# Attention step of a fused kernel: another order of TensorE's work, k and v transposed by halves, positions by wider matmuls

## The chip, the cores and the metric

The kernel runs on one core of a Trainium2 chip. TensorE does matmuls and transposes, VectorE (DVE), ScalarE (ACT) and GpSimd (POOL) do the rest, and SyncE (SP) issues most transfers. Each engine takes its instructions in the order of its own queue and waits where one of them needs something that another engine has not finished. The metric is the device time of one execution in microseconds; lower is better.

## The reference, cut to what matters

Three parts follow each other: attention over pooled keys and values, a mixture of experts that routes each token to one of eight experts, and a dense layer. The change touches the first part and the routing.

```
k_p = k.reshape(B, H, Sp, pool, D).mean(axis=3)      # B, H, S, D = 8, 8, 576, 64; pool = 8
v_p = v.reshape(B, H, Sp, pool, D).mean(axis=3)
scores = scale * np.matmul(q, k_p.transpose(0, 1, 3, 2))
attn = np.exp(scores - np.max(scores)); attn /= np.sum(attn) + 1e-09
x = np.matmul(attn, v_p)                             # then tokens x (heads*D)
logits = x @ w_gate + modality_bias[modality_id]
e_idx = np.argmax(logits, axis=1)                    # a token goes to expert e_idx
out[mask] = gate_w[mask, None] * (relu(x[mask] @ w1[e]) @ w2[e])
g = h * clip(h + 3, 0, 6) / 6, h = out @ w_in;  y = g @ w_out
```

## The kernel before, in words

Attention works on 36 tiles of 128 tokens with all eight heads. A loop written out in Python makes one step for each tile i, and the queues of TensorE, VectorE, ScalarE and SyncE hold the instructions in exactly the order in which the code names them; only GpSimd's order is left to a scheduler. Nine tiles serve two batches. A step is a software pipeline. Its pieces are called by letters here:

- T, `stage_t(i)`: TensorE transposes the exponentials of tile i in five pieces into `tps`, a PSUM tile of two banks with one buffer (pool `ps_t`). ScalarE copies it out to `eT`.
- E, `stage_e(i + 2)`: ScalarE takes the exponential of the differences `d` of tile i + 2, into `e`.
- X, `stage_x`: ScalarE scales the second half of the weighted sums of tile i - 1 by `rs` into `xg`, in four instructions; this frees the PSUM tile `u1`.
- Q, `stage_q(i + 4)`: four transposes of q into `qps`, one PSUM bank with one buffer (pool `ps_q`), copied out by ScalarE to `qT`.
- S, `stage_s(i + 3)`: scores into two buffers `sps` of `ps_s` (three buffers); VectorE takes the maximum `mx` and the difference `d` of each, four instructions.
- A, `stage_a(i)`: weighted sums into the two PSUM tiles `u0` and `u1`, one buffer each; VectorE then makes `rs` and scales the first half into `xg`.

For each batch b the pooled keys and values `kvq` are prepared once, some steps before its first tile. VectorE sums `kv` down to `kvq` in two stages in different steps. `prep(b)` transposes `kvq` with six transposes into `kvps`, which is a buffer of the same pool `ps_t` that T uses; VectorE copies the keys (partitions 0 to 63 of `kvps`) to one half of `bd`, ScalarE copies the same keys to the other half, then two pieces of `bd` to `bp` (`put_p`), and then the values (partitions 64 to 127) to `vT`. One step later `prep2(b)` multiplies `vT` with the gate's weights (`pw`, twelve matmul records on TensorE), and VectorE and GpSimd fill `vb`. `bd` is what S reads, `vb` what A reads.

Routing goes by nine groups of up to five tiles. `route(j)` lists small VectorE instructions (a reduction `l` over `xg`, maximum, one-hot `oh`, and on ScalarE an exponential `ex`), and `run_fill` puts them singly between the larger VectorE instructions of S and A, four in S and four in A. `route_b` adds the positions in an expert's list: for each tile r of the group it sums the one-hots of the earlier tiles with a matrix of ones and its own with a triangular one, 20 matmuls of 8 columns for a group of five. The rows are then scattered to DRAM by GpSimd. At step 28 `first_x` loads the 400 rows of the first expert (`cxg`), GpSimd scales them by the gate (`gate_x`), and TensorE transposes them between the last tiles. From then on the experts and the dense layer follow, which the change doesn't touch.

Of the kernel before, what the change touches and what calls it, by code (L numbers as in the profile page):

```python
# [19 lines left out]
P = 128  # L20
# [32 lines left out]
PQ = (((2, 3), (3, 4)), ((5, 6), (6, 7)))  # L53
PO = 4
QL = 9
# [18 lines left out]
def attention(tc, g, moe, ins, xr_d):  # L74
# [53 lines left out]
    ones = c1.tile([P, P], BF16, name="ones")  # L128
    nc.gpsimd.memset(ones, 1.0)
    tok = c1.tile([P, NTI], F32, name="tok")  # L130
    t9 = tok.rearrange("p (r t) -> p r t", t=9)
# [49 lines left out]
    def kv_ps():  # L181
        return ps_t.tile([P, 1024], F32, name="kvps", tag="t")
# [25 lines left out]

    def prep(b):
        ps = kv_ps()  # L210
        kv_t(b, 2 * D, ps)
        put_k(b, ps)
        put_p(b)
        put_v(b, ps)

# [145 lines left out]
    def route(j):  # L361
# [4 lines left out]
        t = lambda nm, s_, dt=F32: rp.tile(s_, dt, name=nm, tag=nm)  # L366
        l, ex, w, oh = t("l", sh), t("ex", sh), t("w", sh), t("oh", sh, BF16)
        m, m2 = t("m", [P, n, 1]), t("m2", [P, n, 1])
# [3 lines left out]
        def shift():  # L372
            v.tensor_tensor(l, l, m.to_broadcast(sh), op=ALU.subtract)
            nc.scalar.activation(ex, l, AF.Exp)

# [18 lines left out]
        ]  # L394
        if j >= len(GROUPS) - 3:
            return crit[:5] + rest[:1] + crit[5:6] + rest[1:2] + crit[6:] + rest[2:]
        return crit + rest

    def route_b(new=lambda: ps_s.tile([P, 512], F32, name="rps", tag="s")):
        ops = []  # L400
        for j, (x, oh) in list(rt.items()):
            i0, n = GROUPS[j]
            ps = new()
            for r in range(n + 1):
                for r2 in range(min(r + 1, n)):
                    nc.tensor.matmul(ps[:, r * E:(r + 1) * E], tri if r2 == r else ones, oh[:, r2], start=(r2 == 0),
                                     stop=(r2 == min(r, n - 1)))
            ops += route_c(j, ps, *rt.pop(j))
        return ops
# [67 lines left out]
    sched = {}  # L477
    sched2 = {}

# [60 lines left out]
    for b in range(2, B):  # L540
        for w in range(2):
            for n, rs in enumerate(((4,), (2, 1))):
                at2(PQ[b - 2][w][n] if b < 4 else first[b] - 10 + 2 * w + n, lambda b=b, w=w, rs=rs: pool_kv(b, w, v_, rs=rs))
        if b > 2:
            at(first[b] - 12, lambda b=b: (load_kv(b, 0), load_kv(b, 1)))
            at(first[b] - QL, lambda b=b: load_qs(b))
        o = PO if b == 2 else 6 - b % 2
        at(first[b] - o, lambda b=b: prep(b))
        at2(first[b] - o + 1, lambda b=b: prep2(b))
    at2(ZI, zero_rows)  # L550
# [16 lines left out]
    for i in range(NTI - 3):  # L567
# [6 lines left out]
        if i == XL:  # L574
            each(fill)
            each(fill2)
            del fill[:], fill2[:]
            put_rows()
            tc.add_to_no_dep_group("scatter", moe.first_x())
        stage_t(i)  # L580
# [3 lines left out]
        for j, (a, n) in enumerate(GROUPS):  # L584
            if a + n == i:
                fill.extend(route(j))
        if i > 0 and i + 4 < NTI:
            stage_q(i + 4)
        for fn_ in sched.get(i, ()):
            fn_()  # L590
        stage_s(i + 3)
        if i == NTI - 4:
            sp(-1)
        for fn_ in sched2.get(i, ()):
            fn_()
        fill.extend(route_b())
        stage_a(i)
        if i == 0:
            prep_k(1)
            stage_q(4)  # L600
# [181 lines left out]
def moe1(tc, g, xr_d, tok_d, y_d, s_d, w1, w2, w_in):  # L782
# [71 lines left out]
    def first_x():  # L854
        one = lambda j, hi: nc.sync.value_load(g.one[0:1, j:j + 1], min_val=0, max_val=hi)
        s.e0 = one(0, E - 1)
        r0 = one(1, E * R - R + NW)
        i_ = nc.sync.dma_start(s.xg, xr_d[bass.ds(r0, NW)].rearrange("(t p) x -> p t x", p=T4)).ins
        w_dma(s.e0, 0)
# [436 lines left out]
```

## Time and profile before

| | |
|---|---|
| median of three runs | 1419.65 us (1418.83 to 1419.8) |
| the profiled execution's own time | 1420.61 us |
| its span, first to last instruction | 1418.9 us |
| attention, from the first T to the last | 25.3 to 193.3 us |
| granted TensorE clock, mean of the span | 0.993 |

The profiled execution is 0.96 us longer than the median, and 1.71 us of it lie outside the span. A row of the timeline has the start, the duration, the engine, the line, the operation, output and inputs, the count, and in brackets the idle time before it with what ended it. TensorE's rows overlap each other, so what a piece costs is the distance from its start to the start of the next piece.

### The profile page before, as it was taken

The numbers are of one execution on the slowest core, as the hardware profiler recorded it, in microseconds if no ns is written. First come the engines' busy times: TensorE is split into PE (matmuls) and PEld (weight loads), VectorE is DVE, ScalarE is ACT, GpSimd is POOL, SyncE is SP. The second block draws the span as 40 slices with busy tenths as digits, with TensorE's granted clock in tenths as the row PEclk, the third lists the DMA queues.
The fourth block names the chain that finished last, engine by engine and source line by source line (L and its number), as shares of the span: only waits on it lengthen the run. The fifth ranks groups of instructions, "written<-read, shape, count | busy, mean of one in ns | idle before, by whom it ended". The sixth has DMA issues, their size and how long they took to land.

```text
span 1418.9 us, 24229 instructions
## 1 busy us (share of the span) xinstructions
PE 1371.0 (97%) x7685; PEld 1263.2 (89%) x7685; DVE 940.7 (66%) x1922; ACT 624.1 (44%) x1262; POOL 156.5 (11%) x190
## 2 busy tenths in 40 slices
PE   7898999999999999999999999999999999999997
PEld 5787889899999999898888888888889888888886
DVE  6988884888888886777787445645654564455443
ACT  3666663555555554444444333423432342244222
POOL 3232341111111111100000100100010010001001
PEclk8999999999999999999999999999999999999999
DMA  9996265777778776665654544553454355445431
GB/s 247 305 299 190 91 198 161 237 242 242 240 243 248 241 242 199 198 210 179 202 162 119 183 137 123 157 165 114 122 181 141 113 150 176 119 116 166 115 116 67
DMA packets 229238, 253.87 MB, mean 179 GB/s; under 512 B 19225, under 2 KB 191293, under 8 KB 229149
## 3 DMA queue, kind: packets, MB, share of 16 engines
q1 hardware_dynamic: 223388, 232.64, 54.7%
q0 software_dynamic: 5760, 20.10, 3.9%
q8 instruction: 50, 0.82, 0.3%
q14 instruction: 40, 0.32, 0.1%
HBM read 206.21 MB, written 46.47 MB: 178 GB/s over the span
## 4 chain that ended last, share of the span: by engine, by line
issue 56%; POOL 2%; DVE 2%; DMA 1%; PE 1%; ACT 0%; SPq 0%; POOLq 0%; DVEq 0%; ACTq 0%
POOL out_dram L1049 2%; DMA ds<-in_moe_w_out_dram 1%; DVE wl L755 1%; DMA ws<-in_moe_w_dram 0%; PE ph L906 0%; DVE lo L911 0%; PE y L919 0%; DVE da L766 0%; DVE dex L777 0%; DVE dm L764 0%; DVE dm L765 0%; DVE dm L768 0%; SPq L820 0%; ACT dex L763 0%; POOLq L1291 0%
## 5 line engine op out<-in xcount | busy, mean ns | idle before, releaser
L1070 PE MATMUL hps<-yc,sq 128*128 128x384 f32 x2004 | 405.1, 337 | 3.3 <-ACT s L1111 1.6
L1070 PEld LDWEIGHTS hps<-yc,sq 128*128 128x128 f32 x2004 | 358.3, 188 | 37.3 <-ACT s L1111 5.5
L1060 PE MATMUL ops<-wo,gh 128*128 128x512 f32 x1152 | 358.5, 392 | 0.0
L1060 PEld LDWEIGHTS ops<-wo,gh 128*128 128x128 f32 x1152 | 211.4, 188 | 23.1
L1060 PE MATMUL ops<-wo,gl 128*128 128x512 f32 x576 | 228.7, 397 | 0.0
L1082 ACT ACTIVATE r<-c,three 128x384 f32<-128x384 f32 x144 | 88.8, 617 | 208.4 <-DVE c L1092 208.0
L755 DVE TENSOR_TENSOR wl<-ws,wh 128x512 fp32r<-128x512 f32 x192 | 132.8, 728 | 35.5 <-ACT wh L754 32.1
L1086 ACT CAST gh<-r 128x384 fp32r<-128x384 f32 x192 | 98.7, 514 | 129.4 <-DVE r L1083 128.0
L754 ACT CAST wh<-ws 128x512 fp32r<-128x512 f32 x192 | 114.5, 619 | 72.2 <-DMA ws<-in_moe_w_dram 54.4
L919 PE MATMUL y<-lo,wh 128*128 128x400 f32 x384 | 133.6, 348 | 1.8 <-DVE lo L911 1.7
L919 PE MATMUL y<-hi,wh 128*128 128x400 f32 x384 | 134.6, 350 | 0.6 <-ACT hi L910 0.5
L906 PE MATMUL ph<-xhi,wh 128*128 128x400 f32 x384 | 132.3, 344 | 2.0 <-PEq L1291 1.2
L906 PE MATMUL ph<-xlo,wh 128*128 128x400 f32 x384 | 132.8, 346 | 0.0
L906 PE MATMUL ph<-xhi,wl 128*128 128x400 f32 x384 | 132.6, 345 | 0.0
L919 PE MATMUL y<-hi,wl 128*128 128x400 f32 x384 | 132.0, 344 | 0.0
L1060 PEld LDWEIGHTS ops<-wo,gl 128*128 128x128 f32 x576 | 107.9, 187 | 23.1
L1087 DVE TENSOR_TENSOR gl<-r,gh 128x384 fp32r<-128x384 f32 x192 | 106.5, 554 | 27.6 <-ACT gh L1086 23.2
L1049 POOL DMA_INDIRECT out_dram<-osb,tki x36 | 35.3, 982 | 777.3 <-ACT osb L1047 745.4
L1083 DVE SCALAR_TENSOR_TENSOR r<-r,c 128x384 f32<-128x384 f32 x144 | 80.4, 558 | 55.1 <-ACT r L1082 53.2
L829 POOL TENSOR_TENSOR cxg<-cxg 100x512 f32<-100x512 f32 x48 | 56.7, 1184 | 348.4 <-PE ph L906 182.6
L1083 DVE SCALAR_TENSOR_TENSOR r<-r,hps 128x384 f32<-128x384 f32 x48 | 26.6, 554 | 97.7 <-ACT r L1082 97.6
L1082 ACT ACTIVATE r<-hps,three 128x384 f32<-128x384 f32 x48 | 27.9, 581 | 131.6 <-PE hps L1070 131.5
(214 smaller groups left out, 1903.6 us busy)
## 6 DMA issues: line engine op xcount, KB each, us to landing
sq<-sd SPq DMA_DIRECT2D x336, 256.0 KB
ws<-in_moe_w_dram SPq DMA_DIRECT2D x192, 256.0 KB, 3.9
sd<-wq SPq DMA_DIRECT2D x16, 896.0 KB
cxg<-xr SPq DMA_DIRECT2D x44, 225.8 KB
yd<-yo SPq DMA_DIRECT2D x12, 800.0 KB
yr<-yd SPq DMA_DIRECT2D x12, 768.0 KB
kv<-in_k_dram SPq DMA_DIRECT2D x16, 512.0 KB
kv<-in_v_dram SPq DMA_DIRECT2D x16, 512.0 KB
```

What stands on the lines that cost most here:

```text
L754: nc.scalar.copy(hi, src)
L755: nc.vector.tensor_tensor(lo, src, hi.bitcast(F32), op=ALU.subtract)
L829: nc.gpsimd.tensor_tensor(s.xg[:, t, 0:DM].rearrange("p (h x) -> p h x", x=D), v, s.xg[:, t, GC:GC + 1].unsqueeze(2).to_broadcast([T4, H, ...
L906: nc.tensor.matmul(ph, a[j][:, 0, k * P:(k + 1) * P], b[k], start=(n == 0), stop=(n == 11))
L919: nc.tensor.matmul(yps[d], a[j][:, 1, d * P:(d + 1) * P], b, start=(f == 0 and n == 0), stop=(f == 7 and n == 2))
L1049: i_ = nc.gpsimd.indirect_dma_start(out=out, out_offset=bass.IndirectOffsetOnAxis(ap=tki[:, c:c + 1], axis=0), in_=o, in_offset=None).ins
L1060: nc.tensor.matmul(pso[t_], gt[a][:, t * P:(t + 1) * P], wo[f][:, b], start=(q == 0 and fh == th and n == 0), stop=(q == NQ - 1 and fh != ...
L1070: nc.tensor.matmul(ps, w[:, kk, a * P:(a + 1) * P], y[:, b, kk], start=(start and n == 0), stop=(n == 5), skip_group_check=True)
L1082: a_.activation(r, c, AF.Relu, bias=g.three)
L1083: v.scalar_tensor_tensor(r, r, 6.0, c, op0=ALU.min, op1=ALU.mult)
L1086: a_.copy(gh, r)
L1087: late.append(lambda: v.tensor_tensor(gl, r, gh.bitcast(F32), op=ALU.subtract))
```

## The change

Within a step TensorE now does T, then S, then Q, then A. `prep` is split in two: after A of one step three transposes of one half of the heads go into a buffer of `ps_q`, where q's transposes also go, and after A of the next step the other half; each half has its own VectorE copy of keys, ScalarE copy of keys and ScalarE copy of values. `put_p` and `prep2` come in the step after the second half. `PO` becomes 5, so that batch 2 starts its first half one step earlier than its `prep` stood. The one-hots of all groups stay in one tile `ohs` with a column block of zeros behind each group, and the positions of a group are n + 1 matmuls over 8 to 48 columns of it, each shifted by one tile. `route` enters the list behind S and Q instead of ahead of S, but for the group `FE`, and its `ex` is put behind the fifth VectorE instruction in place of the fourth, but for the last three groups. The first expert's rows are loaded by four transfers in place of one.

```diff
-PO = 4
+PO = 5
...
     nc.gpsimd.affine_select(tri, tri, pattern=[[1, P]], compare_op=ALU.is_gt, fill=0.0, base=0, channel_multiplier=-1)
     ones = c1.tile([P, P], BF16, name="ones")
     nc.gpsimd.memset(ones, 1.0)
+    ohs = c1.tile([P, NTI + len(GROUPS), E], BF16, name="ohs")
+    nc.gpsimd.memset(ohs, 0.0)
     tok = c1.tile([P, NTI], F32, name="tok")
     t9 = tok.rearrange("p (r t) -> p r t", t=9)
     for c0, n, b0, cm, p0, p1 in ((0, 4, 0, 4, 0, P), (4, 2, S, 4, 0, P), (7, 2, S + 2, 4, 0, P), (6, 1, 512, 1, 0, 64), (6, 1, S + 512, 1, 64, P)):
...
         kv_t(b, 2 * D, ps)
         put_v(b, ps)
 
-    def prep(b):
-        ps = kv_ps()
-        kv_t(b, 2 * D, ps)
-        put_k(b, ps)
-        put_p(b)
-        put_v(b, ps)
+    def prep(b, z):
+        ps = ps_q.tile([P, 512], F32, name="kvps", tag="q")
+        for c, o in ((4, P - 32 * z), (2 * z, 0), (2 * z + 1, 160)):
+            nc.tensor.transpose(ps[:, o:o + P], kvq[b][:, c], g.idn)
+        k8 = ps[0:64, 0:288].rearrange("p (h k) -> p h k", k=SP)
+        nc.vector.tensor_copy(bd[b % 3][64:128, 4 * z:4 * z + 4, SP:2 * SP], k8)
+        nc.scalar.copy(bd[b % 3][0:64, 4 * z:4 * z + 4, 0:SP], k8)
+        if z == 0:
+            vTs[b] = p2.tile([P, HK], F32, name="vT", tag="vT")
+        nc.scalar.copy(vTs[b][64:128, 288 * z:288 * z + 288], ps[64:128, 0:288])
 
     vTs = {}
 
...
         sh = [P, n, E]
         v = nc.vector
         t = lambda nm, s_, dt=F32: rp.tile(s_, dt, name=nm, tag=nm)
-        l, ex, w, oh = t("l", sh), t("ex", sh), t("w", sh), t("oh", sh, BF16)
+        l, ex, w = t("l", sh), t("ex", sh), t("w", sh)
+        oh = ohs[:, i0 + j:i0 + j + n]
+        late = j < len(GROUPS) - 3
         m, m2 = t("m", [P, n, 1]), t("m2", [P, n, 1])
 
         gs = t("gs", [P, n, 1])
 
         def shift():
             v.tensor_tensor(l, l, m.to_broadcast(sh), op=ALU.subtract)
+            if not late:
+                probs()
+
+        def probs():
             nc.scalar.activation(ex, l, AF.Exp)
 
         def last():
...
             lambda: v.tensor_scalar(gs, gs, 1e-9, None, op0=ALU.add),
             last,
         ]
-        if j >= len(GROUPS) - 3:
+        if not late:
             return crit[:5] + rest[:1] + crit[5:6] + rest[1:2] + crit[6:] + rest[2:]
-        return crit + rest
+        return crit[:5] + [probs] + crit[5:] + rest
 
     def route_b(new=lambda: ps_s.tile([P, 512], F32, name="rps", tag="s")):
         ops = []
         for j, (x, oh) in list(rt.items()):
             i0, n = GROUPS[j]
             ps = new()
-            for r in range(n + 1):
-                for r2 in range(min(r + 1, n)):
-                    nc.tensor.matmul(ps[:, r * E:(r + 1) * E], tri if r2 == r else ones, oh[:, r2], start=(r2 == 0),
-                                     stop=(r2 == min(r, n - 1)))
+            of = ohs[:, i0 + j:i0 + j + n + 1].rearrange("p n e -> p (n e)")
+            for d in range(n + 1):
+                nc.tensor.matmul(ps[:, d * E:(n + 1) * E], ones if d else tri, of[:, 0:(n + 1 - d) * E], start=(d == 0), stop=(d == n))
             ops += route_c(j, ps, *rt.pop(j))
         return ops
 
...
             at(first[b] - 12, lambda b=b: (load_kv(b, 0), load_kv(b, 1)))
             at(first[b] - QL, lambda b=b: load_qs(b))
         o = PO if b == 2 else 6 - b % 2
-        at(first[b] - o, lambda b=b: prep(b))
-        at2(first[b] - o + 1, lambda b=b: prep2(b))
+        for z in range(2):
+            sched1.setdefault(first[b] - o + z, []).append(lambda b=b, z=z: prep(b, z))
+        at2(first[b] - o + 2, lambda b=b: (put_p(b), prep2(b)))
     at2(ZI, zero_rows)
 
     def each(*qs):
...
             each(fill2)
             del fill[:], fill2[:]
             put_rows()
-            tc.add_to_no_dep_group("scatter", moe.first_x())
+            for i_ in moe.first_x():
+                tc.add_to_no_dep_group("scatter", i_)
         stage_t(i)
         stage_e(i + 2)
         if xo:
             stage_x()
         for j, (a, n) in enumerate(GROUPS):
-            if a + n == i:
+            if a + n == i and j == FE:
                 fill.extend(route(j))
-        if i > 0 and i + 4 < NTI:
-            stage_q(i + 4)
         for fn_ in sched.get(i, ()):
             fn_()
         stage_s(i + 3)
+        if i > 0 and i + 4 < NTI:
+            stage_q(i + 4)
+        for j, (a, n) in enumerate(GROUPS):
+            if a + n == i and j != FE:
+                fill.extend(route(j))
         if i == NTI - 4:
             sp(-1)
         for fn_ in sched2.get(i, ()):
             fn_()
         fill.extend(route_b())
         stage_a(i)
+        for fn_ in sched1.get(i, ()):
+            fn_()
         if i == 0:
             prep_k(1)
             stage_q(4)
...
         one = lambda j, hi: nc.sync.value_load(g.one[0:1, j:j + 1], min_val=0, max_val=hi)
         s.e0 = one(0, E - 1)
         r0 = one(1, E * R - R + NW)
-        i_ = nc.sync.dma_start(s.xg, xr_d[bass.ds(r0, NW)].rearrange("(t p) x -> p t x", p=T4)).ins
+        x4 = xr_d[bass.ds(r0, NW)].rearrange("(t p) x -> p t x", p=T4)
+        i_ = [nc.sync.dma_start(s.xg[:, t], x4[:, t]).ins for t in range(4)]
         w_dma(s.e0, 0)
         w_dma(s.e0, 1)
         gate_x()
```

What the queues hold where batch 5 is prepared shows the move. First TensorE's queue before, two steps from one T on (`tps` is T, `qps` Q, `kvps` the transposes of k and v, `sps` S, `ups` A):

```order
L307 MATMUL tps<-idn,e 128x128 x5
L252 MATMUL qps<-idn,q 128x128 x4
L179 MATMUL kvps<-idn,kvq 128x128 x6
L281 MATMUL sps<-bd_134,qT 128x144 x4
L328 MATMUL ups<-vb_130,eT 128x146 x6
L307 MATMUL tps<-idn,e 128x128 x5
L252 MATMUL qps<-idn,q 128x128 x4
L281 MATMUL sps<-bd_134,qT 128x144 x4
L224 MATMUL pw<-wg,vT 128x64 x4
L226 MATMUL pw<-wg,vT 32x64 x2
L328 MATMUL ups<-vb_131,eT 128x146 x6
```

And the same queue now, from A of the step whose end has the first half:

```order
L334 MATMUL ups<-vb_130,eT 128x146 x6
L214 MATMUL kvps<-idn,kvq 128x128 x3
L313 MATMUL tps<-idn,e 128x128 x5
L287 MATMUL sps<-bd_134,qT 128x144 x4
L258 MATMUL qps<-idn,q 128x128 x4
L334 MATMUL ups<-vb_131,eT 128x146 x6
L214 MATMUL kvps<-idn,kvq 128x128 x3
L313 MATMUL tps<-idn,e 128x128 x5
L287 MATMUL sps<-bd_135,qT 128x144 x4
L258 MATMUL qps<-idn,q 128x128 x4
L230 MATMUL pw<-wg,vT 128x64 x4
L232 MATMUL pw<-wg,vT 32x64 x2
```

The six transposes have left the place between Q and S, where they used T's bank, and stand as three and three at the ends of two steps, ahead of the next T; `pw` is a step later. On ScalarE, before, the copies for batch 5 stood behind `qT` of one step, with what each waits for in brackets:

```order
L254 COPY qT<-qps 128x512 [waits PE_49]
L189 COPY bd_135<-kvps 64x8x72 [waits DVE_49]
L192 COPY bp_138<-bd_135 64x4x72
L193 COPY bp_138<-bd_135 64x4x72 [waits Activation_49]
L197 COPY vT<-kvps 64x576
L309 COPY eT<-tps 128x640 [waits PE_49]
```

Now they stand in two steps, each time between `qT` and the next step's `eT`:

```order
L260 COPY qT<-qps 128x512 [waits PE_49]
L217 COPY bd_135<-kvps 64x4x72 [waits DVE_49]
L220 COPY vT<-kvps 64x288
L315 COPY eT<-tps 128x640 [waits PE_49,Activation_49]
L305 ACTIVATE e<-d 128x2x256
L306 ACTIVATE e<-d 128x2x32
L355 ACTIVATE xg<-ups,rs 128x72 x4
```

The copy of keys waits for VectorE in both, and what it waits for has moved. VectorE's queue at that place before, up to the score differences:

```order
L341 TENSOR_TENSOR xg<-ups,rs 128x288
L428 TENSOR_REDUCE pf<-base 128x5
L188 COPY bd_135<-kvps 64x8x72
L283 TENSOR_REDUCE mx<-sps 128x4
L419 CAST ix<-pf 128x5
L286 TENSOR_TENSOR d<-sps,mx 128x2x2x72
```

And now, where the routing's instructions (`base`, `pf`) of an earlier group lie ahead of the copy:

```order
L342 TENSOR_SCALAR rs<-ups 128x4
L436 TENSOR_TENSOR base<-run,rps 128x40
L342 TENSOR_SCALAR rs<-ups 128x4
L437 TENSOR_TENSOR run<-run,rps 128x8
L344 RECIPROCAL rs<-rs 128x8
L438 TENSOR_TENSOR base<-base,ohs 128x40
L347 TENSOR_TENSOR xg<-ups,rs 128x288
L439 TENSOR_REDUCE pf<-base 128x5
L216 COPY bd_135<-kvps 64x4x72
L289 TENSOR_REDUCE mx<-sps 128x4
```

The copy stands behind `rs` and `xg` of the step whose A precedes the half transposes; before, it read transposes that stood ahead of that step's A.

## Rows read from the trace of the kernel before

**Rows 1.** The page's first line: span and instructions.

```profile
span 1418.9 us, 24229 instructions
```

**Rows 2.** Timeline, TensorE, one step without extra work (start, duration, instruction).

```profile
167.67 0.71 PE L307 MATMUL tps<-idn,e 128*128 128x128 f32 x5
168.22 0.60 PE L252 MATMUL qps<-idn,q 128*128 128x128 f32 x4
168.65 1.15 PE L281 MATMUL sps<-bd,qT 128*128 128x144 f32 x8
...
171.53 0.71 PE L307 MATMUL tps<-idn,e 128*128 128x128 f32 x5
```

**Rows 3.** Timeline, ScalarE, the same step.

```profile
168.42 0.69 ACT L309 COPY eT<-tps 128x640 f32<-128x640 f32 x1 [2.23 <-PE tps L307]
...
169.68 0.95 ACT L349 ACTIVATE xg<-ups,rs 128x72 f32<-128x72 f32 x4
```

**Rows 4.** Timeline, VectorE, one step with a stage of pooling.

```profile
126.13 0.46 DVE L283 TENSOR_REDUCE mx<-sps 128x4 f32<-128x288 f32 x1 [0.58 <-PE sps L281]
...
127.93 1.48 DVE L173 TENSOR_TENSOR kv<-kv 128x1280 f32<-128x1280 f32 x1
129.32 0.22 DVE L336 TENSOR_SCALAR rs<-ups 128x4 f32<-128x4 f32 x2
...
130.19 0.45 DVE L283 TENSOR_REDUCE mx<-sps 128x4 f32<-128x288 f32 x1
```

**Rows 5.** Timeline, TensorE, batch 5's `prep` step, its `pw` step and the next.

```profile
113.89 0.71 PE L307 MATMUL tps<-idn,e 128*128 128x128 f32 x5
...
121.59 1.10 PE L224 MATMUL pw<-wg,vT 64*128 64x64 f32 x8
...
122.86 1.76 PE L328 MATMUL ups<-vb,eT 128*128 128x146 f32 x12
124.46 0.71 PE L307 MATMUL tps<-idn,e 128*128 128x128 f32 x5
...
125.44 1.15 PE L281 MATMUL sps<-bd,qT 128*128 128x144 f32 x8
...
128.32 0.71 PE L307 MATMUL tps<-idn,e 128*128 128x128 f32 x5
```

**Rows 6.** Groups by form to 205 us: copies of half the keys.

```profile
L188 DVE COPY bd<-kvps 64x288 f32<-64x288 f32 x2 | 0.9, 451 | 1.4 <-PE kvps L179 1.4
L189 ACT COPY bd<-kvps 64x288 f32<-64x288 f32 x2 | 0.8, 393 | 3.7 <-DVE bd L188 3.7
```

**Rows 7.** Waits to 260 us: who waited for whom, total, times, longest.

```profile
ACT bd L189 <- DVE bd L188: 8.7, 5, 4.0
```

**Rows 8.** Timeline, TensorE: second half of one A.

```profile
174.60 1.01 PE L328 MATMUL ups<-vb,eT 128*128 128x146 f32 x6 [0.19 <-ACT xg L349]
```

**Rows 9.** Timeline, VectorE: the instruction that reads it.

```profile
175.65 0.16 DVE L336 TENSOR_SCALAR rs<-ups 128x4 f32<-128x4 f32 x1 [0.50 <-PE ups L328]
```

**Rows 10.** Waits of TensorE's weight loads, 40 to 200 us.

```profile
PEld L406 <- DVE oh L387: 3.4, 2, 1.9
```

**Rows 11.** Timeline, TensorE: first of 20 position matmuls, and A behind them.

```profile
111.80 0.18 PE L406 MATMUL rps<-oh,tri 128*128 128x8 bf16 x1 [1.67 <-DVE oh L387]
...
112.31 1.74 PE L328 MATMUL ups<-vb,eT 128*128 128x146 f32 x12
```

**Rows 12.** Timeline, GpSimd: the first expert's rows are scaled.

```profile
183.18 4.04 POOL L829 TENSOR_TENSOR cxg<-cxg 100x512 f32<-100x512 f32 x4 [11.32 <-DMA ws<-in_moe_w_dram]
```

**Rows 13.** Timeline, TensorE: those rows are transposed.

```profile
188.41 0.51 PE L837 MATMUL xps<-idn,cxg 100*128 100x100 f32 x4
```

**Rows 14.** Waits of VectorE, 33 to 145 us.

```profile
DVE mx L283 <- PE sps L281: 5.3, 5, 2.5
DVE l L381 <- ACT xg L349: 2.3, 3, 0.9
DVE bd L188 <- PE kvps L179: 1.7, 3, 1.2
```

More of the change, by code (lines that the diff above doesn't have):

```diff
@@ L477, in attention @@
     sched = {}
-    sched2 = {}
+    sched1, sched2 = {}, {}
     def at(i, fn_):
```

## The prediction

> **What bounds the kernel now.** The page's first line gives the span of the profiled execution, 1418.9 us [rows 1]; its own time is 1420.61, 1.71 outside the span and 0.96 over the median. Only attention, 25.3 to 193.3 us, holds edited instructions on the path, so I read the timeline there, engine by engine. The reader should first see the beat of a plain step: T starts at 167.67 and again at 171.53, a period of 3.86 [rows 2]. Which engine sets it? On ScalarE the same step's `eT` starts at 168.42, 0.75 behind T, after 2.23 of idle time ended by TensorE's T; its X ends at 169.68 + 0.95 = 170.63 [rows 3]. From `eT` to the end of X is 2.21, and 0.90 later the next T starts: 0.75 + 2.21 + 0.90 = 3.86. So a plain step is a loop: T, `eT`, X, the second half of A, the next T. A's second half says so itself: it waited for X's `xg` [rows 8].
>
> VectorE has three pieces in a step: M, maxima and differences, 127.93 - 126.13 = 1.80; a stage of pooling, 129.32 - 127.93 = 1.39; R (`rs` and the first half of `xg`), 130.19 - 129.32 = 0.87 [rows 4]. Together 4.06: more than 3.86, so in a step with pooling VectorE is close to being the bound itself. It waits for 9.3 us in the stretch 33 to 145 us, for scores, X and the transposes of k and v [rows 14].
>
> Batch 5's preparation shows what one costs before: the three steps from the T at 113.89 to the T at 128.32 take 14.43 [rows 5], against 3 x 3.86 = 11.58.
>
> **The change part by part.** *Preparation by halves* (six batches, 2 to 7). Before, six transposes stand in T's bank, so the hold falls on the next T until `vT` is copied. Now T's bank is free, and the hold moves to ScalarE: its copy of the keys follows VectorE's copy of the same keys, and behind it in ScalarE's queue stand the values' copy and the next `eT`, which starts the loop above. VectorE's copy now stands behind R of the step (change section, VectorE's queue). I time three steps from T = 0, with pooling on VectorE:
> - S follows T at once, 0.55 behind it (168.22 - 167.67, [rows 2]); the first maximum starts 0.69 behind S (126.13 - 125.44, [rows 4, 5]), so at 1.24. M to 3.04, pooling to 4.43, R to 5.30, half of the keys in 0.45 [rows 6]: 5.75.
> - The next T is at 3.86 plus three transposes, 3 x 0.11 (five take 0.55): 4.19. Its `eT` could start at 4.94, but ScalarE copies keys from 5.75 and values after them, 0.39 each for this size [rows 6]: `eT` at 6.53, X ends at 8.74, T of the third step at 8.74 + 0.90 + 0.33 = 9.97.
> - Second half: VectorE runs M and pooling to 5.75 + 1.80 + 1.39 = 8.94 and waits for A's second half, which starts when X ends and is read 1.05 later (174.60 to 175.65, [rows 8, 9]): 9.79. The rest of R, 0.87 less one of the two `rs` (0.11), ends at 10.55, keys at 11.00, ScalarE's two copies at 11.78.
> - In the third step q's transposes need the bank that this last copy frees: 0.43 (168.65 - 168.22), `pw` 122.86 - 121.59 = 1.27, A 124.46 - 122.86 = 1.60 [rows 2, 5]: the triple ends at 15.08, 0.65 more than 14.43.
>
> Bounds of this: without pooling VectorE still waits for A in the first step (3.07 + 1.05 = 4.12, [rows 2, 8, 9]), 0.42 earlier; carried through, the triple is 14.66, +0.2. On the other side each microsecond by which VectorE starts late shifts the first copy and all behind it, and its work of 4.06 a step leaves nothing to catch up: +2.1 for a triple if it is 1.5 late. Routing instructions stand ahead of about half of the twelve copies. I take +0.9: 6 x 0.9 = **+5.4**.
>
> *Routing later.* The weight loads of the position matmuls waited for `oh` 3.4 us in all, in two places [rows 10], and A stood behind them. Now `oh` is made at least half a step before its matmuls; VectorE's wait of 2.3 for X [rows 14] goes with it. I count **-3.4**, and nothing for VectorE's wait, which lies under the same hold.
>
> *Position matmuls.* 20 take 112.31 - 111.80 = 0.51 [rows 11]. Now six of 8 to 48 columns; no row has such a width in bfloat16, so 6/20 of 0.51 = 0.15 as a value, and 0.51 as the bound if width cost all back. Three groups of five lie in steps where TensorE is awaited: 3 x 0.36 = **-1.1** (0 by the bound). Elsewhere the matmuls stand in the shadow of a preparation.
>
> *S ahead of Q.* In a plain step the loop doesn't pass through either: 0. VectorE gets scores 0.43 earlier, which is worth something only where it is the bound. The cover is ScalarE's loop, and Q's copy, now behind X, has the rest of the step.
>
> *Tail, zero columns, transfers.* Smaller groups lose four or five matmuls each: -0.4 in all, bound 0. The memset of `ohs` is before attention on GpSimd, off the path. The four loads: SP issues three more, with the expert's first weights behind them; GpSimd's four scalings take 183.18 + 4.04 = 187.22, TensorE transposes at 188.41 [rows 12, 13]. So 1.19 covers a later start, and an earlier one gives nothing. If the cover is gone, each microsecond beyond it is lost in full. Batch 2's earlier first half may wait in TensorE's queue for VectorE's pooling of v; before, the transposes could be the late ones (VectorE waited 1.7 for them in three places [rows 14]). I take 0, with +2 as its bound.
>
> Sum: 5.4 - 3.4 - 1.1 - 0.4 = **+0.5**: 1420.61 + 0.5 = 1421.1 for the profiled execution, **1420.2** by the median.
>
> **A rule beside a row.** ScalarE's copy of the keys waits 8.7 us in five places for VectorE's copy of the same keys, 4.0 at most [rows 7]: the two read one bank one behind the other. The Trainium skill, "PSUM — Partial Sum Buffer", section "PSUM bank collisions raise a hardware error", says that two engines must not touch the same bank and the same quadrant of 32 partitions at once, while different quadrants may be read together. For the keys the trace agrees (8.7 us of waits). For the values, partitions 64 to 127, the rule would let ScalarE copy beside VectorE's read; that would hide twelve copies of 0.39, 4.7 us, and the sum would be -4.2. This kernel's ScalarE queue has them behind the copy that waits, so the sum above goes by the queue.
>
> **The rivals.** *Faster: VectorE is on time.* For: 9.3 us of its waits [rows 14] show slack in most steps before, and S now comes 0.43 earlier. Against: 4.06 of work a step. With +0.2 a triple: 1.2 - 4.9 = -3.7, 1416.0. Where those waits were themselves the path and all of them went, less 6 x 0.45 for the six added copies, -6.6 gives 1413.1. It decides where a triple costs less than +0.34.
>
> *Slower: VectorE is late at both copies.* One mechanism: routing and pooling in the same step put the keys' copy about 1.5 late, and ScalarE stalls with `eT` behind it. For: the 4.0 wait of that same copy before [rows 7]. Against: routing also starts later. +2.1 a triple: 12.6 - 4.9 = +7.7, 1427.4. It decides from +1.29 a triple.
>
> *No net change by another way*: the holds of 3.4 were hidden by ScalarE's loop and return as a wait for X, and triples cost the floor: 1.2 - 1.1 - 0.4 = -0.3, 1419.4. It lies within the same band as the forecast.
>
> **How the numbers follow.** About 0.2%, 2.8 us, is what a measurement of this kernel can tell from no change. Forecast 0.36, the no-net-change rival 0.08: together "same" 0.44. VectorE on time 0.30, late 0.26. The range reaches into both sides, from 1413.8 (near the waits gone) to 1426.2 (near two microseconds a triple), leaving out about 1 in 10 at each end.
>
> **What would show it.** In triples, distances from T to T of about 4.2, 5.8 and 5.1, where plain steps stay at 3.86; ScalarE's keys' copy waiting for VectorE's, 0.8 in a first half, with TensorE waiting for `eT`; no wait of weight loads for `oh`; position matmuls of a five-tile group in 0.15 to 0.2; the first expert's transposes not later than the tiles before them allow. I am wrong if VectorE's copy comes before T's end (then ScalarE isn't held, and it is faster), if it comes over 1.5 behind it (slower), or if a step of routing without preparation grows beyond 3.9.

## The result and the profile after

| | before | changed |
|---|---|---|
| median of seven runs | 1419.13 us | 1426.62 us |
| lowest to highest | 1416.24 to 1420.86 | 1424.92 to 1432.42 |
| profiled execution, own time | 1420.61 | 1426.56 |

The ratio is 1.0059, with a 95% interval of 1.0045 to 1.0073: the changed kernel is slower by about 0.6%, 7.5 us between the medians. The forecast was no change that can be measured, and 1426.62 lies just above its range.

The page of the changed kernel begins, where before stood [rows 1]:

```profile
span 1424.8 us, 24068 instructions
```

The spans differ by 5.9 us. The work after attention adds nothing: the last `eT` copy starts at 193.63 us before and at 199.65 now, 6.0 later. The first starts 2.0 earlier now (26.66 and 24.66); this start lies between 23.6 and 26.8 in all the traces of this case. Between the first and the last the changed kernel loses 8.0. The distances from one `eT` copy to the next, read from ScalarE's timeline, show where. `eT` follows T by 0.74 to 0.86 in most steps, but unlike T it shows a hold of ScalarE itself.

| steps | before | now | difference |
|---|---|---|---|
| 4 to 7 (batch 2) | 20.70 | 22.26 | +1.56 |
| 8 to 10 (batch 3) | 15.10 | 18.15 | +3.05 |
| 12 to 14 (batch 4) | 14.94 | 17.28 | +2.34 |
| 17 to 19 (batch 5) | 14.43 | 15.85 | +1.42 |
| 21 to 23 (batch 6) | 15.59 | 18.23 | +2.64 |
| 26 to 28 (batch 7) | 14.42 | 15.47 | +1.05 |
| 11, 15, 16, 20 and 30 (routing) | 23.93 | 19.78 | -4.15 |
| all others, up to the last | | | +0.1 |

The preparations lose 12.1 us and the routing steps gain 4.15. So the loss lies in the preparations, and batch 3's, the dearest, shows it. VectorE's timeline there, in the step whose T starts at 68.75:

```profile
68.73 0.81 DVE L175 TENSOR_TENSOR kv<-kv 128x640 f32<-128x640 f32 x1
69.58 0.49 DVE L175 TENSOR_TENSOR kvq<-kv 128x320 f32<-128x320 f32 x1
...
71.70 0.44 DVE L289 TENSOR_REDUCE mx<-sps 128x4 f32<-128x288 f32 x1
...
73.41 1.48 DVE L175 TENSOR_TENSOR kv<-kv 128x1280 f32<-128x1280 f32 x1
74.81 0.22 DVE L342 TENSOR_SCALAR rs<-ups 128x4 f32<-128x4 f32 x2
75.07 0.20 DVE L344 RECIPROCAL rs<-rs 128x8 f32<-128x8 f32 x1
75.30 0.46 DVE L347 TENSOR_TENSOR xg<-ups,rs 128x288 f32<-128x288 f32 x1
75.79 0.45 DVE L216 COPY bd<-kvps 64x288 f32<-64x288 f32 x1
76.27 0.46 DVE L289 TENSOR_REDUCE mx<-sps 128x4 f32<-128x288 f32 x1
```

This answers [rows 4]. When T starts, VectorE is only beginning the pooling stage of the step ahead (68.73 and 69.58), so the first maximum starts at 71.70, 2.95 behind T. From there VectorE doesn't pause: maxima and differences, a pooling stage of 1.48, `rs`, `xg`, and at last the copy of half of the keys at 75.79. ScalarE's queue in the same stretch:

```profile
71.63 0.61 ACT L260 COPY qT<-qps 128x512 f32<-128x512 f32 x1
76.28 0.39 ACT L217 COPY bd<-kvps 64x288 f32<-64x288 f32 x1 [4.03 <-DVE bd L216]
76.68 0.39 ACT L220 COPY vT<-kvps 64x288 f32<-64x288 f32 x1
77.10 0.70 ACT L315 COPY eT<-tps 128x640 f32<-128x640 f32 x1
```

ScalarE finished `qT` and then waited 4.03 us for that copy. In the kernel before it waited for it in two of these six preparations, 0.38 and 0.65 us; the 4.0 of [rows 7] is the copy at 32.88, in the preparation of batch 1, which the change leaves as it was. Its own copies of keys and values follow, and only then `eT` at 77.10, although its T was done long before, as TensorE's timeline shows:

```profile
73.39 0.49 PE L214 MATMUL kvps<-idn,kvq 128*128 128x128 f32 x3
73.72 0.71 PE L313 MATMUL tps<-idn,e 128*128 128x128 f32 x5
74.27 1.15 PE L287 MATMUL sps<-bd,qT 128*128 128x144 f32 x8
77.13 0.66 PE L258 MATMUL qps<-idn,q 128*128 128x128 f32 x4 [1.72 <-ACT vT L220]
77.90 3.30 PE L334 MATMUL ups<-vb,eT 128*128 128x146 f32 x12
```

T starts at 73.72, S behind it; q's transposes then wait 1.72 for ScalarE's copy out of their bank. The A that follows takes 3.30 where [rows 5] had 1.76; that is the clock, of which more below. The waits of the whole of attention, 25 to 200 us (who waited for whom, total, times, longest):

```profile
ACT bd L217 <- DVE bd L216: 34.2, 12, 4.0
...
PEld qps L258 <- ACT vT L220: 11.9, 11, 2.2
...
PEld L418 <- issue: 0.6, 1, 0.6
```

Twelve halves, twelve waits, 34.2 us in all. Not all of it is loss, since ScalarE has idle time in a plain step too, 2.23 [rows 3]. The last row answers [rows 10]: the weight loads of the position matmuls, which waited 3.4 us for `oh`, now wait 0.6 once, put down to no other engine. The position matmuls of one group, ahead of A, answer [rows 11]:

```profile
118.08 0.19 PE L418 MATMUL rps<-ohs,tri 128*128 128x48 bf16 x1
118.11 0.27 PE L418 MATMUL rps<-ohs,ones 128*128 128x40 bf16 x5
118.24 1.97 PE L334 MATMUL ups<-vb,eT 128*128 128x146 f32 x12
```

A starts 0.16 behind the first of the six, where 20 took 0.51.

### The profile page after: what moved, and what is told of

It reads as the page before. It is cut to its first block, busy times and chain, and to the rows that moved or that the text cites. A ratio compares the mean times of both kernels' runs of the same rounds, so it can differ in the third digit from the quotient of the medians.

```text
span 1424.8 us, 24068 instructions
## 1 busy us (share of the span) xinstructions
PE 1373.6 (96%) x7594; PEld 1263.1 (89%) x7594; DVE 945.7 (66%) x1928; ACT 626.9 (44%) x1274; POOL 155.7 (11%) x191
## 4 chain that ended last, share of the span: by engine, by line
issue 55%; POOL 2%; DVE 2%; PE 1%; DMA 1%; ACT 0%; SPq 0%; POOLq 0%; DVEq 0%; ACTq 0%
POOL out_dram L1068 2%; DVE wl L773 1%; PE y L938 1%; PE ph L925 0%; DMA ws<-in_moe_w_dram 0%; DMA ds<-in_moe_w_out_dram 0%; DVE lo L930 0%; DVE da L784 0%; DVE dex L795 0%; DVE dm L786 0%; DVE dm L782 0%; ACT wh L772 0%; DVE dm L783 0%; POOLq L1310 0%; DVE xlo L773 0%
```

## The experiments

Each kernel was timed beside the kernel before on the same chip. The kernel before itself took 1418.3 to 1418.6 us in the first two sittings and 1424.7 to 1424.8 in the last two, so ratios and differences within a sitting are compared, never levels across them. The second and the fourth sitting were on one and the same chip, so it isn't the chip alone that makes these 6 us, as an expectation below supposes. The theories: by the **queue theory** VectorE's copy of the keys comes late and ScalarE, waiting for it, holds `eT`. By the **bank theory** the loss is q's transposes waiting for their bank. By the **rest theory** the order S ahead of Q, or the routing, loses.

### First sitting: which part, and which wait (before: 1418.57)

**Whole preparation.**

```diff
-PO = 5
+PO = 4
...
-    def prep(b, z):
-        ps = ps_q.tile([P, 512], F32, name="kvps", tag="q")
...
+    def prep(b):
+        ps = kv_ps()
+        kv_t(b, 2 * D, ps)
+        put_k(b, ps)
+        put_p(b)
+        put_v(b, ps)
...
-        for z in range(2):
-            sched1.setdefault(first[b] - o + z, []).append(lambda b=b, z=z: prep(b, z))
-        at2(first[b] - o + 2, lambda b=b: (put_p(b), prep2(b)))
+        at(first[b] - o, lambda b=b: prep(b))
+        at2(first[b] - o + 1, lambda b=b: prep2(b))
```

> The changed kernel with the preparation of k and v whole again, six transposes in T's bank at their old place, and batch 2 at its old step; the order T, S, Q, A, the later routing, the wider position matmuls and the four loads stay. Between the two profiles the steps of a preparation lose 11.9 us and the steps without one gain 4.2. Queue theory (the halves lose: VectorE's copy of the keys comes late and ScalarE waits in front of eT): 1419.1 - 4.2 = about 1415. Rest theory (the halves cost nothing, the order S before Q or the routing loses): stays near 1426.

Measured: 1413.57, ratio 0.9968 (0.9955 to 0.9981). Everything but the halves gains 5 us; the rest theory falls as the cause of the loss.

**Halves only**: the last diff the other way round, in the kernel before.

> The kernel before with nothing but the preparation by halves in q's bank (and batch 2 a step earlier). Queue theory: 1419.1 + 11.9 = about 1431, with ScalarE waiting for VectorE's copy of the keys in up to 12 places. Rest theory: 1417 to 1421.

Measured: 1446.62, ratio 1.0199 (1.0180 to 1.0219): 28 us, more than twice what the queue theory expected. With Q ahead of S a second wait adds itself. TensorE's timeline at one half:

```profile
59.52 0.71 PE L311 MATMUL tps<-idn,e 128*128 128x128 f32 x5
64.36 0.66 PE L256 MATMUL qps<-idn,q 128*128 128x128 f32 x4 [4.14 <-ACT vT L218]
64.86 1.97 PE L285 MATMUL sps<-bd,qT 128*128 128x144 f32 x8
66.76 1.97 PE L228 MATMUL pw<-wg,vT 64*128 64x64 f32 x8
```

The q transposes wait 4.14 us for their bank, and S stands behind them in the queue. So VectorE gets its scores only after the copy that it was late for, and in the next step it is later still. The waits, 25 to 225 us:

```profile
ACT bd L215 <- DVE bd L214: 39.9, 12, 4.6
DVE mx L287 <- PE sps L285: 35.8, 22, 3.0
...
PEld qps L256 <- ACT vT L218: 29.2, 12, 4.4
```

VectorE waited 35.8 us for scores, 22 times, where the kernel before waited 8.0 us, 10 times, in the same window. The S at 64.86 takes 1.97 where 1.15 is usual [rows 2]: the granted clock is at half from 65 to 75 us there.

**Keys on ScalarE**: no copy waits for VectorE any more.

```diff
-        nc.vector.tensor_copy(bd[b % 3][64:128, 4 * z:4 * z + 4, SP:2 * SP], k8)
+        nc.scalar.copy(bd[b % 3][64:128, 4 * z:4 * z + 4, SP:2 * SP], k8)
```

> The changed kernel with both copies of the keys on ScalarE, so that no copy there waits for VectorE; ScalarE has 0.39 to 0.45 us more in each half. Queue theory: the waits (34.2 us in 12 places, of which what lies ahead of T's end costs nothing) go, and of the 11.9 lost at least 6 come back: 1418 to 1421, and no stretch at the half clock. Bank theory (what costs is that q's transposes wait for the bank, whoever copies): the copies take as long as before or longer, so 1425 to 1429.

Measured: 1410.09, ratio 0.9941 (0.9923 to 0.9959), faster than any expectation: more came back than the preparations had lost (16.5 us for 12.1, across sittings). Between 28 and 200 us the granted clock stayed at full, as expected. ScalarE's timeline at batch 3's first half:

```profile
72.93 0.39 ACT L216 COPY bd<-kvps 64x288 f32<-64x288 f32 x1 [1.68 <-PE kvps L214]
73.33 0.39 ACT L217 COPY bd<-kvps 64x288 f32<-64x288 f32 x1
73.73 0.39 ACT L220 COPY vT<-kvps 64x288 f32<-64x288 f32 x1
74.15 0.69 ACT L315 COPY eT<-tps 128x640 f32<-128x640 f32 x1
```

The copies start as soon as the three transposes have landed, and `eT` follows 1.22 behind; in the changed kernel it came 3.38 after T (73.72 to 77.10), here 1.42 (72.73 to 74.15). VectorE is as late as ever in that step (its first maximum 2.96 behind T, its `rs` at 73.81), and no copy waits for it. What ScalarE's copies wait for now, in attention:

```profile
ACT bd L216 <- PE kvps L214: 14.7, 12, 2.8
```

**Pooling behind.** In the steps with a half, VectorE's pooling stands behind the copy of the keys.

```diff
+    cur, behind = [0], []
+    late = behind.append
+    now = lambda f: f()
...
-                at2(PQ[b - 2][w][n] if b < 4 else first[b] - 10 + 2 * w + n, lambda b=b, w=w, rs=rs: pool_kv(b, w, v_, rs=rs))
+                at2(PQ[b - 2][w][n] if b < 4 else first[b] - 10 + 2 * w + n, lambda b=b, w=w, rs=rs: (late if b > 3 and cur[0] in sched1 else now)(lambda: pool_kv(b, w, v_, rs=rs)))
...
+        cur[0] = i
...
         for fn_ in sched1.get(i, ()):
             fn_()
+        while behind:
+            behind.pop(0)()
```

> The changed kernel with VectorE's pooling stage (0.8 to 1.5 us) behind the half copy of the keys instead of ahead of the reciprocal sums, in the steps that have a half. VectorE does the same work. Queue theory: the copy comes up to 1.4 us earlier in each step with pooling and the first half costs nearly nothing; some of it returns a step later because VectorE's total is the same: 1418 to 1423. If VectorE's total work is what counts, not its order: 1425 to 1428. Bank theory: the copies end earlier too, so it expects a gain as well and is not told apart here.

Measured: 1421.53, ratio 1.0021 (1.0006 to 1.0035). VectorE's total work is the same, and the earlier copy is worth something (25 to 225 us):

```profile
ACT bd L217 <- DVE bd L216: 25.8, 11, 3.5
ACT bd L217 <- DVE xg L347: 2.8, 1, 2.8
```

25.8 us, or 28.6 with the twelfth wait, in place of 34.2. That speaks for the order on VectorE and against its total work as the price.

### Second sitting: the other parts alone (before: 1418.31)

**Order only**: S ahead of Q in the kernel before.

```diff
-        if i > 0 and i + 4 < NTI:
-            stage_q(i + 4)
         for fn_ in sched.get(i, ()):
             fn_()
         stage_s(i + 3)
+        if i > 0 and i + 4 < NTI:
+            stage_q(i + 4)
```

> The kernel before with S ahead of Q and nothing else. The prediction took 0 for this order. The kernel with halves and Q ahead of S took 1446.6, with S ahead of Q (and the routing's 4 to 5 us less) 1426.6: with halves the order is worth about 15 us. If the order is worth something only where Q waits for its bank: 1417 to 1420. If VectorE is served earlier in every step: 1410 to 1415.

Measured: 1420.99, ratio 1.0024 (1.0013 to 1.0036), a miss on the slow side: 3 us lost. Its profile has two stretches at half clock, 135 to 139 and 159 to 163 us, and the two steps that hold them are 2.4 us longer than before. The order has a price of its own beside them. In five routing steps ScalarE's copy `qT`, which in the kernel before stood ahead of the routing's `ex`, now stands behind it, and `ex` waits 2.23 to 2.24 us for VectorE's `l`. The next `eT` stands behind both, and these steps (10, 15, 20, 25 and 30) are 0.46 to 0.47 longer. S, now ahead of the next Q, waits for that `qT` too, which it never did before between 25 and 200 us:

```profile
PE sps L281 <- ACT qT L254: 4.5, 4, 1.4
```

With the later routing, in the kernel with the whole preparation, TensorE's matmuls show no such wait.

**Routing only**: the kernel with the whole preparation, with Q ahead of S again (the last diff undone).

> The kernel before with the later routing, the wider position matmuls and the four loads, but with Q ahead of S and the whole preparation. The kernel that has the order S ahead of Q as well took 1413.6. If the order is worth nothing without halves: 1413 to 1415, all of the gain is the routing's (the prediction counted -4.9: 1414). If the order makes the gain: 1418 to 1420.

Measured: 1414.33, ratio 0.9971 (0.9961 to 0.9982). The routing's parts make a gain of about 4 us; with them the order is worth nothing that can be told (0.9968 and 0.9971).

**Half transposes in the scores' pool**, which has three buffers.

```diff
-        ps = ps_q.tile([P, 512], F32, name="kvps", tag="q")
+        ps = ps_s.tile([P, 512], F32, name="kvps", tag="s")
```

> The changed kernel with the half transposes in a buffer of ps_s (three buffers, shared with scores) in place of q's single buffer; VectorE's and ScalarE's queues are the same. Bank theory: q's transposes no longer wait for the copy of values (11.9 us of waits in 11 places), so most of the 11.9 us lost in the preparations comes back: 1416 to 1419. Queue theory: ScalarE still waits for VectorE's copy with eT behind it, q's transposes were only a second victim: 1424 to 1427, at most 2 to 3 us less.

Measured: 1423.44, ratio 1.0040 (1.0026 to 1.0054), between the two expectations and nearer to the queue theory's. The wait for VectorE stays:

```profile
ACT bd L217 <- DVE bd L216: 33.4, 12, 4.0
```

33.4 us beside 34.2, and the first steps of the preparations stay long (7.52 for batch 3, 7.55 in the changed kernel). Only the step behind a preparation gets shorter, 3.86 to 4.12 us in place of 4.22 to 4.37.

**Values first** on ScalarE.

```diff
-        nc.scalar.copy(bd[b % 3][0:64, 4 * z:4 * z + 4, 0:SP], k8)
         if z == 0:
             vTs[b] = p2.tile([P, HK], F32, name="vT", tag="vT")
         nc.scalar.copy(vTs[b][64:128, 288 * z:288 * z + 288], ps[64:128, 0:288])
+        nc.scalar.copy(bd[b % 3][0:64, 4 * z:4 * z + 4, 0:SP], k8)
```

> The changed kernel with ScalarE's copy of the values ahead of its copy of the keys; the values lie in other partitions, so this copy need not wait for VectorE's. Queue theory: 0.39 us less behind the wait in each of twelve halves, at most 4.7 us: 1422 to 1425, and less idle time of ScalarE ahead of the keys' copy by the same. If ScalarE's copy of values waits for VectorE as well: 1426 to 1427.

Measured: 1425.97, ratio 1.0057 (1.0039 to 1.0074), no gain:

```profile
ACT vT L219 <- DVE bd L216: 33.7, 12, 4.0
```

The wait has moved to the values' copy, whole. In this kernel the first of ScalarE's readings of the bank waits for VectorE's, whichever partitions it reads.

### Third sitting: what the wait costs, apart from VectorE's work (before: 1424.65)

The expectations of this sitting were written as times beside a kernel before of 1418 to 1419. It took about 6 us more here, so each is read by its distance from the kernel before.

**Keys on ScalarE, in the scores' pool** (both edits).

> Both edits together: both key copies on ScalarE, and the half transposes in ps_s in place of q's bank. Alone they gave 1410.1 and 1423.4 where the changed kernel has 1426.6. If the hold of q's bank costs by itself (about 3 us, the steps behind a preparation at 3.86 in place of 4.22): 1406 to 1409. If the bank only costs where VectorE's copy is late: 1409 to 1412.

Measured: 1418.12, ratio 0.9953 (0.9940 to 0.9967): 6.5 us faster than before, where by distance the first expectation has 9 to 13 and the second 6 to 10. It fits the second.

**Values on VectorE**: both key copies on ScalarE, the values' copy on VectorE.

```diff
-        nc.scalar.copy(vTs[b][64:128, 288 * z:288 * z + 288], ps[64:128, 0:288])
+        nc.vector.tensor_copy(vTs[b][64:128, 288 * z:288 * z + 288], ps[64:128, 0:288])
```

> The changed kernel with both copies of the keys on ScalarE and the copy of the values on VectorE, so VectorE has as many copies as in the changed kernel (0.45 us a half) and at the same place in its queue, and so late, but nothing that ScalarE has to do for eT stands behind it. Queue theory (the price was eT behind the wait): near the kernel with all copies on ScalarE plus what q's transposes lose by waiting for VectorE: 1411 to 1417. If VectorE's added work or the late release of q's bank is the price: 1420 to 1427.

Measured: 1421.82, ratio 0.9979 (0.9968 to 0.9991): 2.8 us faster than before in that sitting, where the changed kernel is 4.7 to 7.5 slower. ScalarE and then VectorE at batch 3's first half:

```profile
75.00 0.39 ACT L216 COPY bd<-kvps 64x288 f32<-64x288 f32 x1 [1.68 <-PE ups L334]
75.40 0.39 ACT L217 COPY bd<-kvps 64x288 f32<-64x288 f32 x1
75.69 0.69 ACT L315 COPY eT<-tps 128x640 f32<-128x640 f32 x1
```

```profile
76.38 0.46 DVE L347 TENSOR_TENSOR xg<-ups,rs 128x288 f32<-128x288 f32 x1
76.87 0.46 DVE L220 COPY vT<-kvps 64x288 f32<-64x288 f32 x1
```

VectorE's copy stands at the same late place, behind `xg`, and it is `eT` that no longer waits: 75.69, 0.9 behind its T at 74.80. That is the queue theory's test without less work on VectorE: 2.8 us faster than before lies within its 2 to 8. As a time, 1421.82 would lie in the other theory's range, which by distance begins 1 us slower than before. Beside both edits above, 3.7 us are left. q's transposes wait 4.8 us for VectorE's copy in six places; that this makes the 3.7 is likely, and not shown.

**Keys on ScalarE, Q ahead of S.**

> Both key copies on ScalarE, but Q ahead of S again. With VectorE's copy, Q ahead of S took 1446.6 (without the routing's gain of about 4, so some 1442), S ahead of Q 1426.6. If the order matters because scores stand behind the q transposes that wait for a late copy: with prompt copies it costs less than 8: 1411 to 1418. If the order matters by itself: 1423 to 1428.

Measured: 1422.93, ratio 0.9989 (0.9977 to 1.0000). Against keys on ScalarE with S ahead of Q, 5.5 us faster than before in the fourth sitting, Q ahead of S costs some 4 us with prompt copies. With late ones it costs some 16: 28.1 for halves only, less about 4 for the routing that they lack, less the changed kernel's 7.5. Both sums go across sittings and are rough; that S ahead of Q is a shelter from the late copy doesn't hang on their size.

**Whole preparation, keys on ScalarE.**

```diff
-    def put_k(b, ps, zs=(0, 1)):
+    def put_k(b, ps, zs=(0, 1), eng=nc.vector.tensor_copy):
...
-        nc.vector.tensor_copy(bd4[64:128, :, :, SP:2 * SP], k8)
+        eng(bd4[64:128, :, :, SP:2 * SP], k8)
...
     def prep(b):
         ps = kv_ps()
         kv_t(b, 2 * D, ps)
-        put_k(b, ps)
+        put_k(b, ps, eng=nc.scalar.copy)
```

> The kernel with the whole preparation (1413.6) with both key copies of a preparation on ScalarE as well. There ScalarE waited for VectorE's copy only 7.1 us in seven places, of them 4.0 in one that this edit doesn't touch, and T's bank stays held until the values are copied, now behind 0.65 to 0.75 us more of copying on ScalarE. Queue theory: no gain, 1413 to 1417: moving the copy pays only where it frees ScalarE from a wait. If less work for VectorE is what made the gain with halves: 1408 to 1411.

Measured: 1419.35, ratio 0.9957 (0.9944 to 0.9969), beside 0.9968 for the whole preparation: the intervals overlap. Nothing clear is gained where there was hardly a wait to remove.

### Fourth sitting: side by side (before: 1424.82)

**The changed kernel again.**

> The changed kernel itself, on the same chip as the next three. It was 7.5 us slower than the kernel before; the chips differ by some 6 us in the kernel before, so here again 6 to 9 us slower than before, whatever the level.

Measured: 1429.50, ratio 1.0033 (1.0018 to 1.0049), 4.7 us: less than expected, still slower. The granted clock never fell within attention here, so the loss doesn't need it.

**Keys on ScalarE again.**

> Both key copies on ScalarE, beside the changed kernel on one chip. Queue theory: 14 to 18 us less than the changed kernel in the same rounds, 7 to 10 less than before. If the 16.5 us came from comparing two chips: under 12.

Measured: 1419.29, ratio 0.9962 (0.9946 to 0.9977): 10.2 us less than the changed kernel in the same sitting. Across sittings it had been 16.5 (1426.62 and 1410.09). 10.2 is under the 12 at which the expectation puts part of that down to comparing sittings: the size depends on the sitting, the sign doesn't. The traces show where. From the first to the last `eT` the changed kernel took 174.99 us in its first trace and 175.93 in this sitting, the kernel with keys on ScalarE 159.75 and 171.04. Its 11.3 lie in eleven steps, 0.6 to 1.7 in each. Two of them, within 33 to 37 and 84 to 88 us, ran at half clock. In others an engine was released later, as VectorE's `vb` of one batch here, in the first sitting and in this one:

```profile
99.45 0.23 DVE L241 TENSOR_TENSOR vb<-pw,mk 128x64 f32<-128x64 f32 x1 [0.33 <-PE pw L232]
```

```profile
106.65 0.22 DVE L241 TENSOR_TENSOR vb<-pw,mk 128x64 f32<-128x64 f32 x1 [2.51 <-PE ups L334]
```

Why one kernel has these waits in one sitting and not in the other is not shown.

**Keys on ScalarE, in the scores' pool, again.**

> Both key copies on ScalarE and the half transposes in ps_s. If holding q's bank costs by itself, 2 to 4 us less than both key copies on ScalarE alone; if it cost only where VectorE's copy was late: the same within 1 us.

Measured: 1419.27, ratio 0.9960 (0.9947 to 0.9974), no difference that can be told from 1419.29: with prompt copies the bank costs nothing that shows.

**Keys on ScalarE, pooling behind.**

> Both key copies on ScalarE, and VectorE's pooling behind A's reciprocals in the steps with a half. With VectorE's copy of the keys that move gave 4 to 5 us, because it brought the copy earlier. Queue theory: with no copy on VectorE to wait for, nothing is left to bring earlier: within 2 us of both key copies on ScalarE alone. If VectorE's order counts by itself (weighted sums freed earlier): 3 to 5 us less.

Measured: 1418.77, ratio 0.9959 (0.9944 to 0.9973): within 2 us, as the queue theory has it.

## Why the prediction was wrong

**The mechanism was named, its price was mis-sized.** "VectorE's copy now stands behind R of the step" and "ScalarE copies keys" behind it, with "the next `eT`" behind that, is what the trace shows and what the copies on ScalarE removed. The step that failed is the first line of the triple: "the first maximum starts 0.69 behind S ... so at 1.24". Behind T it started at 3.41, 2.95, 2.72, 1.24, 2.57 and 2.40 us in the first halves of batches 2 to 7. Only batch 5, from which the rows came, had VectorE on time. The keys' copy ended 7.89, 7.49, 7.44, 6.00, 7.40 and 6.25 behind T, for 5.75 worked out. From `eT` to `eT` the prediction's triple is 5.78 + 5.25 + 4.05 = 15.08; the mean one is 7.03 + 5.90 + 4.26 = 17.19, so most of the miss is in the first half. Against before the preparations lost 12.1 in place of the 5.4 in the sum, 2.0 each, not 0.9. That is the rival "VectorE is late at both copies", with +2.1 a triple and 1427.4, to which I gave 0.26.

What makes VectorE late is the step ahead of the triple, which the prediction didn't work out: it starts the triple with VectorE free. In batches 2, 3, 4 and 6 a pooling stage of the step ahead is still to be done when T starts or just then ending, and there the keys' copy ends 7.40 to 7.89 behind T. Batches 5 and 7 have no such stage, and there it ends at 6.00 and 6.25. The rival's "routing and pooling in the same step" names the right work, but not the step ahead from which it comes, and its support was misread: the 4.0 of [rows 7] stands in no preparation that the change edits.

It could have been read before. VectorE's and TensorE's timelines of the kernel before, at the start of the step of batch 3's preparation:

```profile
69.13 0.81 DVE L173 TENSOR_TENSOR kv<-kv 128x640 f32<-128x640 f32 x1
```

```profile
69.12 0.71 PE L307 MATMUL tps<-idn,e 128*128 128x128 f32 x5
```

The pooling stage of the step ahead starts with T there, and with T or behind it in the preparations of batches 2, 4 and 6 as well, but not in those of 5 and 7. The kernel before doesn't care: its copy of the keys stood between two tiles' pieces in VectorE's queue (batch 3's at 71.58, after 0.23 of waiting for the transposes), and its T waited for the bank, 0.69 until the values were copied, not for R. I took the one batch whose rows I had as a template for six, and the 4.06 of VectorE's work against a period of 3.86, which the prediction states, already said that VectorE does not catch up in such steps. The bound, "+2.1 for a triple if it is 1.5 late", was the likely case.

**The gains were right.** The routing's holds, the position matmuls and the tail were put at -4.9; the routing steps gained 4.15 in the trace, and the kernels with everything but the halves came out 4.0 and 5.0 us faster than before. Position matmuls: 0.15 expected, 0.16 measured.

**S ahead of Q at 0** holds for the sum, since the halves were worked out in that order, but the sentence on its cover was incomplete: the order also keeps VectorE's scores out of the wait for q's bank. Without it the halves cost 28 us. Alone in the kernel before it lost about 3 us, which the prediction did not have: "the loop doesn't pass through either" leaves out ScalarE's queue in a routing step, where `qT` came to stand behind `ex` and ahead of `eT`, and S waited for it.

**Transfers and zero columns at 0**: GpSimd's last scaling of the first expert's rows ends at 186.94 us in the changed kernel, and TensorE transposes the first rows at 194.43; the cover is larger than the 1.19 before.

**The copy of values.** The 4.7 us that the Trainium skill's rule on banks and quadrants ("PSUM — Partial Sum Buffer", "PSUM bank collisions raise a hardware error") would give were rightly left out: with the values first, ScalarE waited 33.7 us all the same. Whether the chip would let both read at once was not tried; the wait here is one of the program.

**The rival "no net change"** and "VectorE is on time" fall with the twelve waits.

**What stays open**: why the same kernel before takes 6 us more in two of the sittings, why the kernel with keys on ScalarE lost more there than the changed one, and how the 3 us of the order alone divide between clock and wait.

## What to carry to other kernels

A copy that is split between two engines, one behind the other, puts the second engine's whole queue at the mercy of the first one's place in its own: before splitting such a step, look at how late the first engine is in each of the steps concerned, not in one of them, and what the step ahead leaves it to do. If an engine's work in a step exceeds the period, work out the step with that engine late. Here giving both copies to the engine that needs them, 0.39 us more work for it in each half, turned +0.3% to +0.6% into -0.4% to -0.6%, the best version found; another bank or the pooling behind gave nothing on top of it, and Q ahead of S took most of it back. That the halves are then worth anything beside the whole preparation with the same routing (-0.3% to -0.4%) is not shown clearly: the intervals touch.

## What the runs showed of the hardware that was not expected

TensorE's granted clock fell to the lower level (1.2 GHz, 0.50) inside attention, which it did not in the profile of before after its first 30 us. The changed kernel, two stretches (start and end, length, busy times, then the granted clock, the third figure from the end):

```profile
75.00:82.00 7.00, 5.16 (x27) 4.37 (x26) 4.96 (x14) 3.48 (x10) 3.80 (x4) 0.76 1.03 318
...
146.00:150.00 4.00, 3.59 (x16) 3.58 (x17) 2.08 (x10) 1.12 (x4) 0.00 (x0) 0.57 0.00 0
```

The same kernel in the fourth sitting:

```profile
75.00:82.00 7.00, 4.51 (x32) 3.87 (x32) 5.59 (x15) 4.08 (x12) 3.34 (x4) 1.00 1.07 341
...
146.00:150.00 4.00, 3.45 (x29) 3.06 (x27) 3.21 (x12) 2.29 (x7) 1.01 (x1) 1.00 0.00 0
```

In the first profile the clock fell at about 78 us, after TensorE had waited 1.72 at 75.4, and at about 146 us, after a wait of 2.00 that ended at 144.17. In the other the same waits, 1.71 and 2.00, stood ahead of the same A and the clock stayed. So such a wait doesn't decide it alone; what does is not shown. The price can be read by laying the two beside each other: from `eT` to `eT` 6.38 and 5.56 us in batch 3's second step, 6.40 and 5.66 in batch 6's. That is 0.82 and 0.74, of which the step behind the second gives back 0.38 (4.37 and 4.75): 1.2 to 1.6 of the 12.1 us. In the kernel with halves only, whose profiled execution was its slowest (1450.90), five stretches within attention, one of them ten microseconds long, ran at half.
